# Weight conversion and input splitting moved from VectorE to GpSimd in a fused attention + two-MLP kernel

## The chip, the cores and the metric

One NeuronCore of a Trainium2 chip runs the whole program. The metric is the device time of one execution in microseconds; the table below has the median of three. The engines are named as in the profile: PE (TensorE matmuls) with PEld (its weight loads), DVE (VectorE), ACT (ScalarE), POOL (GpSimd) and SP, which issues the DMAs. Each engine works off its own queue strictly in the order in which the program was written; engines wait for one another through semaphores.

## The reference

Three stages, each fed by the one before; 3072 tokens of 384 features.

```
attention: y_t = q_t S;  S += beta_t k_t (v_t - S k_t)      # 4 batches x 8 heads, 768 steps
first MLP:  h = x @ w_in          # 384 -> 2048
            g = (a0 + a1 h + a2 h^2 + a3 h^3) / (1 + |b0||h| + |b1| h^2 + 1e-6)
            x = g @ w_out         # 2048 -> 384
second MLP: h = x @ w_in2;  out = (h tanh(softplus(h))) @ w_out2
```

The MLP weights arrive as 64-bit floats and have to be converted on the chip.

## The kernel before, in words

Tokens are kept in six groups of 512. An MLP is a sequence of **units**: one unit is one group (512 tokens) times one slice of 128 hidden features, so each MLP has 6 x 16 = 96 units, numbered 0 to 95 in the first MLP and on from 96 in the second. Units 16, 32, 48, 64 and 80 begin a new group. Products are formed from two parts of each number, a high part in the fast fp32r format and the remainder ("low half"), so a unit is 9 matmuls up (L893) and 9 down (L1002).

In the first MLP the work of unit u between its two matmul blocks is a chain over three engines. With the letters of the list that orders it:

- 1a (ACT, L924): q = |h|, read from PSUM; 1c (ACT, L933): s = a3 h + a2.
- 1b: r = b1 q + b0. On POOL (L927) for the units in `m1.pool`, else on ACT (L931).
- 1d (POOL, L937): q = q r, the denominator less 1.
- 1e, 1f (ACT, L945 and L947): r = exp(-ln(q + 1 + 1e-6)), its reciprocal; ACT issues them in the next unit's round, just ahead of 1a of that unit.
- 1g, 1h (DVE, L952 and L954): s = (s h + a1) h. 1h is the last reader of h and frees its PSUM buffer; there are two, so the up matmuls of unit u+2 wait for 1h of unit u.
- 1i, 1j, 1k (DVE, L961 to L970): the quotient g; 1L (ACT, L904) its high part; 1m (POOL, L908) its low part.

One round of the loop writes, for all engines, the list

```
"fx fw y0 y1 1e 1f u0 u1 u2 1a 1b 1c 1i 1j 1k 1d 1g 1h y2 d0 d1 d2 d3 xa 1L 1m xB f c",
```

where y0 to y2 copy a finished group's three sums out of PSUM (ACT, L1124, in the round of units 20, 36, 52, 68 and 84), xa and xB split the next group's input x into its high (ACT, L873) and low half (L877), fx loads it, and c and f advance the conversion of the second MLP's weights, a step here and there. A side (half) of a weight slice goes through these steps: its magnitude on ACT (L739, `mag`), a clamp (L744) and a shift (L748) on DVE (`size`), sign and low word on DVE (`sign` L754, `low` L760), then the high part on ACT (L767, `out`) and the remainder on POOL (L772, `rest`). The first 16 sides are converted during units 7 to 88 of the first MLP, one step in a unit, in the units listed in `calm`. A magnitude is put into the queue in the round after the `size` of the side before; `out` and `rest` in the round after `low`. The order on POOL at a round's end is 1m, then xB if POOL has it, then what f flushes.

The functions that the diff touches:

Of the kernel before, what the change touches and what calls it, by code (L numbers as in the profile page):

```python
# [9 lines left out]
F32 = mybir.dt.float32  # L10
F32R = mybir.dt.float32r
I32 = mybir.dt.int32
I64 = mybir.dt.int64
ACTF = mybir.ActivationFunctionType
ALU = mybir.AluOpType
# [27 lines left out]
CONV_START, CONV_RATE = 6, 4  # L43
# [650 lines left out]
class Weights:  # L694
# [5 lines left out]
    LEAST = 2.0 ** -15  # L700
    MOST = 1.875 * 2.0 ** 16
    free = False
    word = None

    def __init__(self, nc, w_in, w_out, sb, kept, passing, scratch):
# [14 lines left out]
    def convert(self, f, side):  # L720
        nc = self.nc
        w = {}

        def get():
            w["raw"] = self.sb.tile([128, 3, 128], I64, "w64")
            src = self.w_out[f * 128:(f + 1) * 128] if side else self.w_in[:, :, f * 128:(f + 1) * 128]
            nc.sync.dma_start(out=w["raw"], in_=src)

        def word(i):
            return w["raw"].rearrange("p k c -> p (k c)").bitcast(I32).rearrange("p (n t) -> p n t", t=2)[:, :, i]  # L730

        def mag():
            w["m"] = self.sb.tile([128, 384], I32, "wm")
            if self.free:
                nc.vector.tensor_scalar(
                    out=w["m"], in0=word(1), scalar1=0x7FFFFFFF, scalar2=None, op0=ALU.bitwise_and
                )
            else:
                nc.scalar.activation(out=w["m"].bitcast(F32), in_=word(1).bitcast(F32), func=ACTF.Abs)  # L739

        def size():
            m = w["m"]
            w["x"] = m if self.word is None else self.word.bitcast(I32)
            nc.vector.tensor_scalar(  # L744
                out=w["x"].bitcast(F32), in0=w["m"].bitcast(F32), scalar1=self.LEAST, scalar2=self.MOST,
                op0=ALU.max, op1=ALU.min,
            )
            nc.vector.tensor_scalar(  # L748
                out=w["x"], in0=w["x"], scalar1=3, scalar2=0x3FFFFFF8,
                op0=ALU.logical_shift_left, op1=ALU.bitwise_and,  # L750
            )

        def sign():
            nc.vector.scalar_tensor_tensor(  # L754
                out=w["x"], in0=word(1), scalar=-(1 << 30), in1=w["x"],
                op0=ALU.bitwise_and, op1=ALU.bitwise_or,
            )

        def low():
            nc.vector.scalar_tensor_tensor(  # L760
                out=w["m"], in0=word(0), scalar=29, in1=w["x"],
                op0=ALU.logical_shift_right, op1=ALU.bitwise_or,
            )

        def out():
            m = w["m"].bitcast(F32).rearrange("p (k c) -> p k c", k=3)
            nc.scalar.copy(out=self.tile(f)[:, 0, side], in_=m)  # L767

        def rest():
            t = self.tile(f)  # L770
            m = w["m"].bitcast(F32).rearrange("p (k c) -> p k c", k=3)
            nc.gpsimd.tensor_tensor(out=t[:, 1, side], in0=m, in1=t[:, 0, side].bitcast(F32), op=ALU.subtract)  # L772

        def done():
            if side and f in self.tag:
                self.store(f)

        return get, mag, size, sign, low, out, rest, done

    def plan(self, p, fs):  # L780
# [265 lines left out]
def tile_delta_attention_two_mlps(  # L1046
# [14 lines left out]
    nc = tc.nc  # L1061
# [24 lines left out]
    units = [(g, f) for g in range(NG) for f in range(NF)]  # L1086
    n1 = len(units)
    units += [(g, f) for g in range(NG) for f in range(NF)]
    n2 = len(units)
# [3 lines left out]
    w2 = Weights(nc, moe2_w_in, moe2_w_out, sb, (), range(DIRECT), wd[1])  # L1093
    def run(fns):
        for fn in fns:
            fn()
# [3 lines left out]
    m1 = Mlp1(nc, w1, sb, ps, x1, consts)  # L1100
    m2 = Mlp2(nc, w2, sb, ps, x2, consts)

    def mlp(i):
        return m1 if i < n1 else m2

    def starts(i):
        return i == 0 or i == n1 or units[i][0] != units[i - 1][0]
# [70 lines left out]
    with ExitStack() as bctx:  # L1178
        sb2 = bctx.enter_context(tc.tile_pool(name="sb2", bufs=1, reuse_waits="tile"))
        ps2 = bctx.enter_context(tc.tile_pool(name="ps2", bufs=1, space=PSUM, reuse_waits="tile"))  # L1180
        sb.add(sb2, w=NF - FQ - FG, wt=1, w64=1, wm=1, x=1, q=3, s=3, r=2, g=3, gh=5 - FIRST, ev=3)
        ps.add(ps2, h=2, o=4, r=2)
        own = FQ + FG
        fetch_w = {n: (w1.fetch_split, own + LOOK + n) for n in range(NF - own - LOOK)}
        for f in range(DIRECT):
            fetch_w[n1 - NF + 6 + f] = (w2.fetch_split, f)
        calm = [i for i in range(CONV_START, n1 - 8) if not any(starts(i + 5 - k) for k in range(3))]
        for f in range(LOOK):
            w1.fetch_split(own + f)
        steps = [  # L1190
            (m1, "1a", m1.e1, [0]), (m1, "1b", m1.e1, [1]), (m1, "1c", m1.e1, [2]), (m1, "1d", m1.e2, None),
            (m1, "1e", m1.e3, [0]), (m1, "1f", m1.e3, [1]), (m1, "1g", m1.e4, [0]), (m1, "1h", m1.e4, [1]),
            (m1, "1i", m1.e5, [0]), (m1, "1j", m1.e5, [1]), (m1, "1k", m1.e5, [2]),
            (m1, "1l", m1.hi, "V"), (m1, "1L", m1.hi, "A"), (m1, "1P", m1.hi, "P"),
            (m1, "1m", m1.lo, "P"), (m1, "1M", m1.lo, "V"),
            (m2, "2a", m2.e1, None), (m2, "2b", m2.e2, None), (m2, "2M", m2.lo, None),
        ]
        steps = {name: (m, f, a) for m, name, f, a in steps}
        ups, downs = {}, {}
        m1.pool = {i for i in range(n1) if i % 2 or any(starts(j) for j in range(i + 3, i + 6) if j < n2)}  # L1200
        m2.pool = range(n1, n1 + NF)
        for i in range(n2 + max(LG.values())):
            kind = int(i >= n1)
            if i == CONV_START - 3:
                conv.start()

            def at_x(f):
                for k in range(3):
                    j = i + 5 - k
                    if 0 < j < n2 and starts(j):  # L1210
                        f(mlp(j))(units[j][0], k)

            for op in LISTS[kind]:
                if op in steps:
                    m, f, a = steps[op]
                    j = i - LG[op[0] + {"L": "l", "P": "l", "M": "m"}.get(op[1], op[1])]
                    if FIRST <= j < n2 and mlp(j) is m:
                        f(j, *([a] if a else []))
                elif op[0] == "u" and FIRST <= i < n2:
                    if i not in ups:  # L1220
                        ups[i] = mlp(i).up(i, *units[i])
                    n = int(op[1])
                    run(ups[i][3 * n:3 * n + 3])
                elif op[0] == "d" and 0 <= i - FIRST < FIRST:
                    if i - FIRST not in downs:
                        downs[i - FIRST] = down(i - FIRST)
                    n = int(op[1])
                    run(downs[i - FIRST][0][3 * n:3 * n + 3])
                elif op[0] in "dvy" and FIRST <= i - LAG - (op[0] == "y") < n2:
                    j = i - LAG - (op[0] == "y")  # L1230
                    if j not in downs:
                        downs[j] = down(j)
                    n = int(op[1])
                    if op[0] == "d":
                        run(downs[j][0][3 * n:3 * n + 3])
                    elif (op[0] == "y") == (j < n1):
                        run(downs[j][1][n:n + 1])
                elif op == "fw" and i in fetch_w:
                    fetch, f = fetch_w[i]
                    fetch(f)  # L1240
                elif op == "fx" and i + 8 < n2 and starts(i + 8):
                    mlp(i + 8).fetch_x(units[i + 8][0])
                elif op == "xa":
                    at_x(lambda m: m.x_hi)
                elif op == "xB":
                    at_x(lambda m: lambda g, k: m.x_lo(g, k, "V"))
                elif op == "c" and i > n1:
                    w2.free = True
                    w2.word = w2.word or ps.tile([128, TOK], F32, "r")[:, 0:384]
                    conv.pull(CONV_RATE)  # L1250
                elif op == "c" and i in calm:
                    conv.pull(6 * DIRECT * (calm.index(i) + 1) // len(calm) - conv.n)
                elif op == "f":
                    conv.flush()
# [29 lines left out]
```

## Time and profile before

| | before |
|---|---|
| median of 3 runs | 1126.9 us (1125.48 to 1130.12) |
| profiled execution | 1126.43 us |
| its span, first to last instruction | 1124.7 us |
| PE, DVE, ACT, POOL busy over the span | 1060.0, 720.8, 610.8, 541.2 us |

The profiled execution's own time is 1.7 us above its span, which lies before the first and behind the last instruction. Attention fills the first 319 us, the first MLP reaches to about 726 us, the second from there to the end. In the first MLP DVE is busy more than nine tenths, ACT and POOL between seven and nine tenths; in the second DVE, ACT and POOL are mostly idle and PE is busy throughout.

### The profile page before, as it was taken

What the parts mean: (1) busy time and instruction counts of PE and PEld (TensorE: products, weight loads), DVE (VectorE), ACT (ScalarE), POOL (GpSimd) and SP (SyncE); (2) the same over time, 40 slices, a digit from 0 to 9 for tenths busy, and PEclk for the clock granted to TensorE, in tenths of its full rate; (3) what the DMA queues carried; (4) which work ended last, traced back from release to release, by engine and by line L of the source; (5) the groups of instructions that cost most, each with busy time, mean ns of one, the idle gap of its engine ahead of it and who ended that gap; (6) DMA issues with size and microseconds to landing.
All of it is one profiled execution on the core that took longest, in us unless ns stands there. A gap on an engine that the chain in (4) does not pass through costs nothing.

```text
span 1124.7 us, 24637 instructions
## 1 busy us (share of the span) xinstructions
PE 1060.0 (94%) x10172; PEld 920.8 (82%) x10172; DVE 720.8 (64%) x1207; ACT 610.8 (54%) x1100; POOL 541.2 (48%) x623
## 2 busy tenths in 40 slices
PE   6778988798989999999999999999999999999998
PEld 5668877688868778878887887899999999999997
DVE  5996577995669999999999999992121211212110
ACT  4524455233568888988889888743333223233322
POOL 4287778667447777777777877763000000000000
PEclk8996899995899999999999999999999999999999
DMA  7616877234473021121202036250101001010000
GB/s 146 140 29 163 201 206 199 46 88 101 102 267 141 15 99 43 57 71 62 94 15 98 15 141 239 67 172 1 57 1 57 1 11 46 1 57 1 29 1 28
DMA packets 120111, 92.91 MB, mean 83 GB/s; under 512 B 79680, under 2 KB 104384, under 8 KB 120000
## 3 DMA queue, kind: packets, MB, share of 16 engines
q1 hardware_dynamic: 119744, 91.25, 27.7%
q8 instruction: 79, 1.29, 0.5%
q14 instruction: 32, 0.26, 0.1%
q0 software_dynamic: 256, 0.10, 0.1%
HBM read 63.02 MB, written 28.31 MB: 81 GB/s over the span
## 4 chain that ended last, share of the span: by engine, by line
PE 50%; POOL 15%; DVE 12%; ACT 12%; issue 7%; DMA 3%; SPq 2%; POOLq 0%; DVEq 0%; ACTq 0%
PE h L893 20%; PE o L1035 18%; POOL q L937 7%; POOL gh L908 3%; PE o L1002 3%; ACT r L945 3%; POOL r L927 3%; PE c_ps L597 2%; ACT q L924 2%; ACT r L947 2%; PE y_ps L635 2%; DVE tmp L520 1%; SPq L310 1%; PE c_ps L580 1%; PE s_all L620 1%
## 5 line engine op out<-in xcount | busy, mean ns | idle before, releaser
L893 PE MATMUL h<-x,w 128*128 128x512 f32 x1278 | 318.0, 393 | 3.9 <-DVE s L954 3.6
L893 PEld LDWEIGHTS h<-x,w 128*128 128x128 f32 x1278 | 237.0, 188 | 56.5 <-DVE s L954 10.2
L908 DVE TENSOR_TENSOR gh<-g,gh 128x512 fp32r<-128x512 f32 x80 | 55.3, 692 | 282.8 <-ACT g L1026 282.8
L1021 ACT ACTIVATE gh<-h 128x512 fp32r<-128x512 f32 x96 | 57.5, 599 | 231.4 <-PE h L893 231.4
L1035 PE MATMUL o<-w,gh 128*128 128x384 f32 x864 | 162.5, 337 | 0.0
L1002 PE MATMUL o<-gh,w 128*128 128x512 f32 x648 | 159.2, 390 | 0.0
L1035 PEld LDWEIGHTS o<-w,gh 128*128 128x128 f32 x864 | 153.4, 188 | 6.0
L908 POOL TENSOR_TENSOR gh<-g,gh 128x512 fp32r<-128x512 f32 x110 | 142.6, 1297 | 23.8 <-ACT g L1026 21.4
L937 POOL TENSOR_TENSOR q<-q,r 128x512 f32<-128x512 f32 x94 | 122.0, 1297 | 61.6 <-ACT r L931 57.2
L1002 PEld LDWEIGHTS o<-gh,w 128*128 128x128 f32 x648 | 121.5, 188 | 26.0 <-ACT ev L1124 0.8
L893 PE MATMUL h<-x,wg 128*128 128x512 f32 x432 | 107.0, 392 | 2.8 <-DVE wm L760 1.6
L893 PEld LDWEIGHTS h<-x,wg 128*128 128x128 f32 x432 | 80.5, 188 | 19.9 <-DVE s L954 2.5
L945 ACT ACTIVATE r<-q,cst 128x512 f32<-128x512 f32 x94 | 65.0, 692 | 48.8 <-POOL q L937 48.7
L933 ACT ACTIVATE s<-h,ab 128x512 f32<-128x512 f32 x94 | 72.7, 774 | 0.0
L954 DVE SCALAR_TENSOR_TENSOR s<-s,ab,h 128x512 f32<-128x512 f32 x94 | 70.2, 747 | 3.3
L961 DVE SCALAR_TENSOR_TENSOR q<-q,r 128x512 f32<-128x512 f32 x94 | 63.8, 679 | 13.4 <-ACT r L947 13.1
L965 DVE SCALAR_TENSOR_TENSOR r<-s,ab,r 128x512 f32<-128x512 f32 x94 | 70.1, 745 | 0.0
L526 POOL TENSOR_TENSOR xs<-xs,tmp 128x30 f32<-128x30 f32 (+14 forms) x120 | 63.1, 526 | 9.4
L952 DVE TENSOR_TENSOR s<-s,h 128x512 f32<-128x512 f32 x94 | 63.8, 679 | 4.6 <-ACT s L933 4.6
L970 DVE SCALAR_TENSOR_TENSOR g<-q,r 128x512 f32<-128x512 f32 x94 | 64.5, 687 | 3.2
L520 POOL TENSOR_TENSOR tmp<-xs 128x30 f32<-128x30 f32 (+14 forms) x120 | 59.2, 493 | 7.4
L904 ACT CAST gh<-g 128x512 fp32r<-128x512 f32 x94 | 58.5, 623 | 0.0
(157 smaller groups left out, 1696.7 us busy)
## 6 DMA issues: line engine op xcount, KB each, us to landing
w<-w SPq DMA_DIRECT2D x24, 768.0 KB, 7.0
w<-in_moe_w_in_dram SPq DMA_DIRECT2D x32, 384.0 KB, 3.6
w<-in_moe_w_out_dram SPq DMA_DIRECT2D x32, 384.0 KB, 3.3
xraw<-x SPq DMA_DIRECT2D x36, 256.0 KB, 4.1
w<-wt SPq DMA_DIRECT2D x8, 768.0 KB, 3.4
kn<-in_k_dram SPq DMA_DIRECT2D x48, 96.0 KB, 3.6
gh<-in_q_dram SPq DMA_DIRECT2D x48, 96.0 KB, 3.3
v<-in_v_dram SPq DMA_DIRECT2D x48, 96.0 KB, 3.9
```

What stands on the lines that cost most here:

```text
L520: eng.tensor_tensor(out=tv, in0=ls[:, j, j + 1:HC].unsqueeze(1).to_broadcast([128, j, n]), in1=xs[:, 0:j, j:j + 1].to_broadcast([128, j, n ...
L893: self.nc.tensor.matmul(out=self.st[i]["h"], lhsT=self.w.t[f][:, a, 0, k], rhs=self.x[g][:, b, k], start=(n == 0), stop=(n == 8),)
L908: (nc.gpsimd if engine == "P" else nc.vector).tensor_tensor(out=s["gh"][:, 1], in0=s["g"], in1=s["gh"][:, 0].bitcast(F32), op=ALU.subtract)
L933: nc.scalar.activation(out=s["s"], in_=s["h"], func=ACTF.Identity, scale=k["a3"], bias=k["a2"])
L937: nc.gpsimd.tensor_tensor(out=s["q"], in0=s["q"], in1=s["r"], op=ALU.mult)
L945: nc.scalar.activation(out=s["r"], in_=s["q"], func=ACTF.Ln, bias=k["c"])
L952: nc.vector.tensor_tensor(out=s["s"], in0=s["s"], in1=s["h"], op=ALU.mult)
L954: nc.vector.scalar_tensor_tensor(out=s["s"], in0=s["s"], scalar=k["a1"], in1=s["h"], op0=ALU.add, op1=ALU.mult)
L965: nc.vector.scalar_tensor_tensor(out=s["r"], in0=s["s"], scalar=k["a0"], in1=s["r"], op0=ALU.add, op1=ALU.mult)
L970: nc.vector.scalar_tensor_tensor(out=s["g"], in0=s["q"], scalar=2.0, in1=s["r"], op0=ALU.subtract, op1=ALU.mult, reverse0=True)
L1002: self.nc.tensor.matmul(out=self.acc[g][d], lhsT=self.w.t[f][:, a, 1, d], rhs=self.st[i]["gh"][:, b], start=(first and n == 0), stop=(last ...
L1035: self.nc.tensor.matmul(out=self.acc[g][t][:, 0:384], lhsT=self.st[i]["gh"][:, a, t * 128:(t + 1) * 128], rhs=self.w.t[f][:, b, 1].rearran ...
```

## The change

In the second MLP's weights, while they are converted during the first MLP (`ahead`), the clamp leaves DVE: POOL does it right behind the magnitude, in place, and `size` on DVE is the shift alone. The low halves of x for groups 1 to 5 of the first MLP go from DVE to POOL; they, and the high halves on ACT, stand in rounds 7, 5 and 3 ahead of the group's first unit (all odd) in place of 5, 4 and 3. POOL does 1b in odd units only; before it also did in units 12, 28, 44, 60, 76 and 92. x is loaded 12 units ahead in place of 8. `calm` now leaves out the two rounds in which sums are or have just been copied out (20 and 21, 36 and 37, ...), and no longer those in which x is split, so the conversion steps stand in other units than before. The first group's x and all of the second MLP (its first group's x, split in rounds 91 to 93, included) keep DVE and the old distances.

```diff
--- before.py
+++ after.py
@@ -700,6 +700,7 @@
     LEAST = 2.0 ** -15
     MOST = 1.875 * 2.0 ** 16
     free = False
+    ahead = False
     word = None
 
     def __init__(self, nc, w_in, w_out, sb, kept, passing, scratch):
@@ -737,16 +738,21 @@
                 )
             else:
                 nc.scalar.activation(out=w["m"].bitcast(F32), in_=word(1).bitcast(F32), func=ACTF.Abs)
+            if self.ahead:
+                clamp(nc.gpsimd, w["m"])
+
+        def clamp(engine, out):
+            engine.tensor_scalar(
+                out=out.bitcast(F32), in0=w["m"].bitcast(F32), scalar1=self.LEAST, scalar2=self.MOST,
+                op0=ALU.max, op1=ALU.min,
+            )
 
         def size():
-            m = w["m"]
-            w["x"] = m if self.word is None else self.word.bitcast(I32)
+            w["x"] = w["m"] if self.word is None else self.word.bitcast(I32)
+            if not self.ahead:
+                clamp(nc.vector, w["x"])
             nc.vector.tensor_scalar(
-                out=w["x"].bitcast(F32), in0=w["m"].bitcast(F32), scalar1=self.LEAST, scalar2=self.MOST,
-                op0=ALU.max, op1=ALU.min,
-            )
-            nc.vector.tensor_scalar(
-                out=w["x"], in0=w["x"], scalar1=3, scalar2=0x3FFFFFF8,
+                out=w["x"], in0=w["m"] if self.ahead else w["x"], scalar1=3, scalar2=0x3FFFFFF8,
                 op0=ALU.logical_shift_left, op1=ALU.bitwise_and,
             )
 
@@ -1184,7 +1190,7 @@
         fetch_w = {n: (w1.fetch_split, own + LOOK + n) for n in range(NF - own - LOOK)}
         for f in range(DIRECT):
             fetch_w[n1 - NF + 6 + f] = (w2.fetch_split, f)
-        calm = [i for i in range(CONV_START, n1 - 8) if not any(starts(i + 5 - k) for k in range(3))]
+        calm = [i for i in range(CONV_START, n1 - 8) if not any(starts(i - 4 - k) for k in range(2))]
         for f in range(LOOK):
             w1.fetch_split(own + f)
         steps = [
@@ -1197,18 +1203,22 @@
         ]
         steps = {name: (m, f, a) for m, name, f, a in steps}
         ups, downs = {}, {}
-        m1.pool = {i for i in range(n1) if i % 2 or any(starts(j) for j in range(i + 3, i + 6) if j < n2)}
+        m1.pool = range(1, n1, 2)
         m2.pool = range(n1, n1 + NF)
         for i in range(n2 + max(LG.values())):
             kind = int(i >= n1)
             if i == CONV_START - 3:
                 conv.start()
+                w2.ahead = True
 
             def at_x(f):
                 for k in range(3):
+                    j = i + 7 - 2 * k
+                    if 0 < j < n1 and starts(j):
+                        f(m1)(units[j][0], k)
                     j = i + 5 - k
-                    if 0 < j < n2 and starts(j):
-                        f(mlp(j))(units[j][0], k)
+                    if n1 <= j < n2 and starts(j):
+                        f(m2)(units[j][0], k)
 
             for op in LISTS[kind]:
                 if op in steps:
@@ -1238,14 +1248,16 @@
                 elif op == "fw" and i in fetch_w:
                     fetch, f = fetch_w[i]
                     fetch(f)
-                elif op == "fx" and i + 8 < n2 and starts(i + 8):
-                    mlp(i + 8).fetch_x(units[i + 8][0])
+                elif op == "fx":
+                    for j in ((i + 12,) if i + 12 < n1 else ()) + ((i + 8,) if n1 <= i + 8 < n2 else ()):
+                        if starts(j):
+                            mlp(j).fetch_x(units[j][0])
                 elif op == "xa":
                     at_x(lambda m: m.x_hi)
                 elif op == "xB":
-                    at_x(lambda m: lambda g, k: m.x_lo(g, k, "V"))
+                    at_x(lambda m: lambda g, k: m.x_lo(g, k, "P" if m is m1 else "V"))
                 elif op == "c" and i > n1:
-                    w2.free = True
+                    w2.free, w2.ahead = True, False
                     w2.word = w2.word or ps.tile([128, TOK], F32, "r")[:, 0:384]
                     conv.pull(CONV_RATE)
                 elif op == "c" and i in calm:
```

How the instructions move, in two places. POOL, from 1d of unit 11 on (wt and wm are weight tiles, x and xraw the split and the loaded input); before:

```order
L937 TENSOR_TENSOR q<-q,r 128x512
L908 TENSOR_TENSOR gh<-g,gh 128x512
L772 TENSOR_TENSOR wt<-wm,wt 128x384
L927 TENSOR_SCALAR r<-q,ab 128x512
L937 TENSOR_TENSOR q<-q,r 128x512
L908 TENSOR_TENSOR gh<-g,gh 128x512
```

The same place after the change, where all lines have larger numbers (1d L943, 1m L914, 1b L933, the low half L883, `rest` L778, the clamp L745):

```order
L943 TENSOR_TENSOR q<-q,r 128x512
L914 TENSOR_TENSOR gh<-g,gh 128x512
L883 TENSOR_TENSOR x<-xraw,x 128x512
L778 TENSOR_TENSOR wt<-wm,wt 128x384
L943 TENSOR_TENSOR q<-q,r 128x512
L914 TENSOR_TENSOR gh<-g,gh 128x512
L745 TENSOR_SCALAR wm<-wm 128x384
```

Ahead of 1d of unit 12 there stood a `rest` and 1b; now a low half of x and a `rest`, and 1b has gone to ACT. A clamp stands behind unit 12's 1m.

ACT, from 1a of unit 11 to 1e of unit 12 (q is written by 1a, s by 1c, gh by 1L); before:

```order
L924 ACTIVATE q<-h 128x512
L933 ACTIVATE s<-h,ab 128x512
L873 CAST x<-xraw 128x512
L904 CAST gh<-g 128x512
L767 CAST wt<-wm 128x384
L945 ACTIVATE r<-q,cst 128x512
L947 ACTIVATE r<-r 128x512
L924 ACTIVATE q<-h 128x512
L933 ACTIVATE s<-h,ab 128x512
L873 CAST x<-xraw 128x512
L904 CAST gh<-g 128x512
L945 ACTIVATE r<-q,cst 128x512
```

After the change, from 1a of unit 12 (L930) on:

```order
L930 ACTIVATE q<-h 128x512
L937 ACTIVATE r<-q,ab 128x512
L939 ACTIVATE s<-h,ab 128x512
L910 CAST gh<-g 128x512
L740 ACTIVATE wm<-w_4949 128x384
L951 ACTIVATE r<-q,cst 128x512
```

Unit 11 keeps its high half of x and its `out`; in unit 12 the high half is gone, and 1b and a magnitude have come.

Where the moved steps stand in units 6 to 94, which are 89, read off the same orders. The 15 low halves on POOL stand in units 9, 11, 13, 25, 27, 29 and so on. Of the 16 `rest`, eight stand in even units before (18, 22, 26, 38, 42, 80, 84, 88) and eight after (20, 26, 42, 46, 62, 66, 82, 88); of the eight in odd units four now stand directly behind a low half of x (11, 57, 73, 77). The 17 magnitudes, each with its clamp on POOL now, stand in even units seven times before (8, 50, 66, 70, 74, 82, 86) and eight times after (8, 12, 28, 32, 48, 52, 68, 74); of the nine in odd units two (43, 59) have a low half ahead of the clamp. The third copy of sums, y2, in the round of an even unit, shares that unit with an `out` in unit 84 before and in unit 20 after, and with a magnitude in units 52 and 68 after. The first two copies share an odd unit with a magnitude or an `out` in 19 and 35 before and in 35, 51 and 83 after.

## Rows read from the trace of the kernel before

**Rows 1.** Busy time by stretch: us, PE, PEld, DVE, ACT, POOL, clock, DMA

```profile
333.60:726.10 392.50, 389.14 (x1692) 315.50 (x1693) 373.11 (x557) 337.56 (x574) 298.70 (x258) 1.00 0.24 84
726.10:1124.70 398.60, 393.68 (x1981) 357.24 (x1980) 100.83 (x158) 125.93 (x241) 31.87 (x27) 1.00 0.11 35
```

**Rows 2.** Waits in 333.6 to 726.1: total us, times, longest

```profile
ACT r L945 <- POOL q L937: 46.1, 70, 1.3
PEld h L893 <- DVE s L954: 12.7, 22, 2.1
```

**Rows 3.** Timeline of PE: start, us, the up matmuls of two units

```profile
564.11 2.20 PE L893 MATMUL h<-x,w 128*128 128x512 f32 x9
...
568.18 2.20 PE L893 MATMUL h<-x,w 128*128 128x512 f32 x9
```

**Rows 4.** Timeline of ACT and POOL, units 62 and 63; idle time before in brackets

```profile
572.18 0.59 ACT L924 ACTIVATE q<-h 128x512 f32<-128x512 f32 x1
...
573.70 1.30 POOL L937 TENSOR_TENSOR q<-q,r 128x512 f32<-128x512 f32 x1 [1.52 <-ACT r L931]
...
576.25 0.59 ACT L924 ACTIVATE q<-h 128x512 f32<-128x512 f32 x1
...
577.02 0.77 POOL L927 TENSOR_SCALAR r<-q,ab 128x512 f32<-128x512 f32 x1 [0.77 <-ACT q L924]
```

**Rows 5.** Timeline of ACT: 1a of unit 6 and of unit 95

```profile
338.14 0.59 ACT L924 ACTIVATE q<-h 128x512 f32<-128x512 f32 x1
...
709.83 0.59 ACT L924 ACTIVATE q<-h 128x512 f32<-128x512 f32 x1
```

**Rows 6.** Timeline of ACT: 1a of units 50, 51, 52 and 53

```profile
522.48 0.60 ACT L924 ACTIVATE q<-h 128x512 f32<-128x512 f32 x1
...
526.66 0.59 ACT L924 ACTIVATE q<-h 128x512 f32<-128x512 f32 x1
...
530.83 0.59 ACT L924 ACTIVATE q<-h 128x512 f32<-128x512 f32 x1
...
535.05 0.60 ACT L924 ACTIVATE q<-h 128x512 f32<-128x512 f32 x1
```

**Rows 7.** Timeline of ACT: 1a of units 13 and 14

```profile
367.81 0.59 ACT L924 ACTIVATE q<-h 128x512 f32<-128x512 f32 x1
...
371.90 0.59 ACT L924 ACTIVATE q<-h 128x512 f32<-128x512 f32 x1
```

**Rows 8.** Timeline of ACT: 1a of units 23, 24 and of 26, 27, 28

```profile
409.56 0.59 ACT L924 ACTIVATE q<-h 128x512 f32<-128x512 f32 x1
...
414.07 0.59 ACT L924 ACTIVATE q<-h 128x512 f32<-128x512 f32 x1
...
422.32 0.59 ACT L924 ACTIVATE q<-h 128x512 f32<-128x512 f32 x1
...
426.47 0.60 ACT L924 ACTIVATE q<-h 128x512 f32<-128x512 f32 x1
...
430.75 0.59 ACT L924 ACTIVATE q<-h 128x512 f32<-128x512 f32 x1
```

**Rows 9.** Timeline of ACT: 1a of units 84 and 85

```profile
663.67 0.59 ACT L924 ACTIVATE q<-h 128x512 f32<-128x512 f32 x1
...
668.30 0.59 ACT L924 ACTIVATE q<-h 128x512 f32<-128x512 f32 x1
```

**Rows 10.** Groups of lines in 333.6 to 726.1: count, busy us, mean ns

```profile
L927 POOL TENSOR_SCALAR r<-q,ab 128x512 f32<-128x512 f32 x52 | 40.6, 781 | 32.0 <-ACT q L924 32.0
...
L772 POOL TENSOR_TENSOR wt<-wm,wt 128x384 fp32r<-128x384 f32 x16 | 17.6, 1101 | 0.0
L877 DVE TENSOR_TENSOR x<-xraw,x 128x512 fp32r<-128x512 f32 x18 | 16.4, 908 | 0.0
...
L744 DVE TENSOR_SCALAR wm<-wm 128x384 f32<-128x384 f32 x16 | 10.6, 664 | 0.0
```

**Rows 11.** Group 0's low half of x on POOL: min/median/max ns

```profile
L877 POOL TENSOR_TENSOR x<-xraw,x x3: 1268/1271/1272, 280.1 to 290.4; 128x512 fp32r<-128x512 f32 x3
```

More of the change, by code (lines that the diff above doesn't have):

```diff
@@ L739, in mag, with size @@
                 nc.scalar.activation(out=w["m"].bitcast(F32), in_=word(1).bitcast(F32), func=ACTF.Abs)
-        def size():
-            m = w["m"]
-            w["x"] = m if self.word is None else self.word.bitcast(I32)
-            nc.vector.tensor_scalar(
-                out=w["x"].bitcast(F32), in0=w["m"].bitcast(F32), scalar1=self.LEAST, scalar2=self.MOST,
+            if self.ahead:
[3 more added lines that the diff above has]
+                out=out.bitcast(F32), in0=w["m"].bitcast(F32), scalar1=self.LEAST, scalar2=self.MOST,
                 op0=ALU.max, op1=ALU.min,
             )
+        def size():
+            w["x"] = w["m"] if self.word is None else self.word.bitcast(I32)
+            if not self.ahead:
+                clamp(nc.vector, w["x"])
             nc.vector.tensor_scalar(
-                out=w["x"], in0=w["x"], scalar1=3, scalar2=0x3FFFFFF8,
+                out=w["x"], in0=w["m"] if self.ahead else w["x"], scalar1=3, scalar2=0x3FFFFFF8,
                 op0=ALU.logical_shift_left, op1=ALU.bitwise_and,
```

## The prediction

> **What bounds the kernel now.** I first ask where time can be gained at all. By the stretches, the second MLP keeps PE busy 393.7 of 398.6 us, at a granted clock of 1.00, with all other engines mostly idle [rows 1]: nothing that happens there moves the end. The first MLP is the place: PE has 3.4 us idle in 392.5, but idle is not all that it loses. A unit's up matmuls begin 4.08 us apart where nothing holds them [rows 3], and 89 units of that are 363.1 us. How long did 89 units take?
>
> The list of waits names two suspects for the first MLP. PE's weight loads wait for 1h on DVE, 22 times, 12.7 us [rows 2], and DVE is busy 373.1 of 392.5 us [rows 1]. That reads as if DVE were the bound. But the same list has ACT waiting for POOL's 1d 70 times, 46.1 us [rows 2], on a chain that also repeats in each unit: 1a, 1b, 1d, 1e, 1f, and only then, since ACT's queue is in order, 1a of the next unit. To tell the two apart I read the starts of 1a. In an even unit, with 1b on ACT, the next 1a comes after 4.07 us [rows 4]; in an odd one, with 1b on POOL, after 4.17 (unit 51 to 52, [rows 6]). The mean, 4.12, is above PE's 4.08, so the chain alone is slower than PE. From 1a of unit 6 to 1a of unit 95 it takes 371.7 us [rows 5] for 89 units, 4.18 each, which is 8.6 us above PE's 363.1. In each of these 89 intervals 1a follows the end of 1f directly; none is ended by h from PE or by anything on DVE. So the reader should see in DVE's 12.7 us an echo: 1h trails a chain that is late by itself, and PE trails 1h. DVE's own delays shift a stall of PE by a unit or two and are then absorbed, because PE can regain 0.09 us where the chain cannot.
>
> So I count what the change does to this chain, in units 6 to 94.
>
> **The chain before, as base and extras.** Base: 39 even units with 1b on ACT at 4.07 us; 38 units with 1b on POOL behind such a unit at 4.17; and 12 units with 1b on POOL behind another such unit, which take 4.09 [rows 7]. Sum 158.7 + 158.5 + 49.1 = 366.3. Measured 371.7, so conversion, splitting and copies now cost the chain 5.4 us. Their prices, where a row isolates one:
> - A magnitude in an even unit: 4.18 against 4.07, 0.11 (unit 50 to 51, [rows 6]). In odd units ACT has room: unit 51, with two copies of sums, takes the plain 4.17 [rows 6].
> - y2 in an even unit: 4.22, 0.15 [rows 6]; y2 with an `out`: 4.63, 0.56 [rows 9].
> - `out` and `rest` in an even unit: that unit 4.15 (0.08), the next 4.28 (0.11; units 26 and 27, [rows 8]), together 0.19; with a two-step `size` on DVE alongside, the next takes 4.51 (unit 23, [rows 8]), together 0.42.
>
> **Removed from DVE.** 16 clamps, 10.6 us, and 15 of 18 low halves, 15 x 0.908 = 13.6 us [rows 10]: 24 us of DVE. I credit the chain with nothing for them. DVE's queue still decides how soon 1h follows 1a, but the end comes from the last unit where PE waits, and there (units 92 to 94) DVE still splits x as before. What hides this work is the chain itself; with a faster chain it would count, up to the 8.6 us above.
>
> **Base after.** 45 even units at 4.07, 44 odd at 4.17: 183.2 + 183.5 = 366.6, 0.3 more than before, because the pairs of POOL units at 4.09 are gone.
>
> **Added to POOL: low halves of x.** One takes 1.27 us there [rows 11]. In an undisturbed pair POOL finishes 1m of the odd unit just as the even unit's 1a begins (idle 1.52 us up to 573.70, so from 572.18, where 1a starts) [rows 4]. So a low half at an odd unit's end falls into a gap of 1.52 us and by itself costs nothing, with 0.25 to spare: nine of the fifteen stand so. Four have a `rest` behind them, mean 1.10 us [rows 10]: 1.27 + 1.10 - 1.52 = 0.85 late for 1d of the even unit, 3.4 us in all. This is the largest term. Two have a clamp behind them: with the clamp at 0.59 (below), 1.27 + 0.59 - 1.52 = 0.34, 0.7 in all.
>
> **Added to POOL: clamps.** The trace has none on POOL. The nearest row is 1b there, also one input and two scalar operations, 0.781 us for 512 columns [rows 10]; for 384 I take three quarters, 0.59. Lower bound: nothing. Upper bound: the price of a two-input step of 384 columns, 1.10 [rows 10]. In an odd unit it has the 1.52 gap. In an even one POOL is idle 0.77 us before the next 1b [rows 4], so 0.59 fits at no cost; at 1.10 it would not, by 0.33. VectorE waits for a clamp only at the very first `size`, which was put right behind its magnitude; that can delay 1h of unit 8 by about 1 us, once, and PE regains it.
>
> **Moved by `calm`.** Eight `rest` in even units before, eight after. After: unit 20 shares its y2 with an `out`, 0.6; the seven others cost 0.19 (four, no `size` alongside) or between that and 0.42 (three, the shift alone alongside; I take 0.30): 1.7. y2 with a magnitude in units 52 and 68: I take the 0.56 of y2 with `out` plus 0.04 for the longer step, 1.2. Magnitudes in 8, 28, 32 and 48: 0.4; in 12 and 74 they hide behind the late 1d. y2 alone in 36 and 84: 0.3. Three odd units with a weight step and two copies: at most y2's 0.15 each, 0.4. Unit 92, now with 1b on ACT and a high half of x there: 0.2.
>
> **x loaded sooner.** The DMAs go past one weight fetch, for a unit eleven places on; x is used five units later. Nothing waits for either in the rows; zero, and if the weight were late, it would stall PE once at unit 15.
>
> **Sum.** Extras after: 3.4 + 0.7 + 0.6 + 1.7 + 1.2 + 0.4 + 0.3 + 0.4 + 0.2 = 8.9 us. Change: 8.9 - 5.4 + 0.3 = +3.8 us. Against the profiled execution that is 1126.43 + 3.8 = 1130.2; the median of the runs lies 0.5 above it. I take **1130.5 us**, 0.3% more: less than the 0.5% (5.6 us) that a measurement of this kernel can tell from no change.
>
> **A rule beside the rows.** The same subtraction takes 0.908 us on DVE in this stretch and 1.27 on POOL [rows 10, 11]. The Trainium skill (GPSIMD Engine Reference, Engine selection) calls POOL about two times slower for two-input elementwise steps and about line rate for one input. By its factor the low half would be an estimated 1.8 us and each of the fifteen would outgrow the 1.52 gap: nine by 0.3 and the six crowded ones by 0.55 more than above, some 6 us on top, 1136. The trace has POOL at 1.4 times, and I go by the trace.
>
> **Rivals.**
> 1. *DVE does bind* (faster). For: 12.7 us of waits name it and it is 95% busy. Against: 1a never waits for it in 89 units. If PE really ran behind DVE alone, the loss above PE's pace, 8.6 us, could go: 1117.8 at best, about 1122 with half. It decides where a 1a starts later than the end of 1f. Chance 0.10.
> 2. *The gaps take everything* (no change). If 1d's wait has more room than the two units that I read, the six crowded places cost nothing: 8.9 - 4.1 = 4.8 us of extras, -0.3 in all, 1126.2 to 1126.6. Against: in rows 4 the gap is closed by ACT's 1b, a fixed step. Chance 0.13.
> 3. *POOL's steps are dearer* (slower). Clamps at 1.10 us: six even units at 0.33 and two crowded ones at 0.51 more, 3.0 us. Every even `rest` at 0.42: 1.3. Sum 1130.5 + 4.3 = 1134.8. For: `rest` has a mean of 1.10 and unit 23 shows 0.23 more than unit 27 when DVE's tensor-scalar steps lie alongside. Against: the change takes half of those steps away. Chance 0.15. The Trainium skill (SBUF, Who interferes with whom) has a cause that would press this way: VectorE and GpSimd share a port pair, and the second to start is blocked until the first ends. By that rule more POOL work meets DVE's shifts; the spread of the rows agrees.
>
> **Range and chances.** The forecast has 0.62. Its own range is 1128.5 to 1132.5 (extras 7 to 11). To hold 8 in 10 the range reaches rival 2 and most of rival 3: 1125.8 to 1134.0. Faster by over 0.5% (below 1121.3): 0.09, rival 1; slower by over 0.5% (above 1132.5): 0.17, most of rival 3 and the forecast's upper edge; within: 0.74.
>
> **What would show it.** In the changed kernel: 1a to 1a still 4.07 and 4.17 in plain units, and 1a behind 1f everywhere; units 12, 58, 74 and 78 at about 4.9; 44 and 60 at about 4.4; 52 and 68 at about 4.7; DVE busy some 24 us less in the first MLP with PE's total hardly moved; POOL's clamp near 0.6 us. I am wrong if 1a begins to wait for PE or DVE, if low half plus `rest` does not delay 1d, or if clamps take over 0.77 us.

## The result, and the profile after

The changed kernel takes 1139.2 us, median of 6 runs (1133.1 to 1145.8), against 1127.0 for the kernel before; the ratio is 1.0117, 95% interval 1.007 to 1.0164. The forecast was 1130.5 with a range to 1134.0: the time lies outside it, on the slow side. Slower was the direction; the amount, 12.2 us, is more than three times the 3.8 that I had. The execution of e4 that was profiled, used below, is a slow one of its kernel, but from 345 to 700 us its granted clock is 1.00 as in the others, so that stretch can be compared.

The profiled execution takes 1138.44 us, 12.0 more than that of before. The chain of the prediction is the place to look first. Timeline of ACT in the changed kernel, 1a (now L930) of unit 6 and of unit 95:

```profile
338.91 0.59 ACT L930 ACTIVATE q<-h 128x512 f32<-128x512 f32 x1
...
722.04 0.59 ACT L930 ACTIVATE q<-h 128x512 f32<-128x512 f32 x1
```

That is 383.1 us for the same 89 units that took 371.7 [rows 5]: +11.4, where the whole execution differs by 12.0; 0.8 had come before unit 6, and what differs behind unit 95 is under 0.5. From the first down matmul of the second MLP to the last instruction both kernels take 393.0 us. So the loss is the chain's.

The stretch and the waits of the first MLP (columns as in [rows 1, 2]), and the groups on POOL (count, busy us, mean ns, as in [rows 10]):

```profile
334.40:738.50 404.10, 395.63 (x1692) 312.80 (x1693) 359.54 (x526) 342.77 (x580) 340.24 (x284) 1.00 0.23 82
```

```profile
ACT r L951 <- POOL q L943: 52.2, 71, 2.0
DVE q L967 <- ACT r L953: 35.4, 42, 1.9
...
PEld h L899 <- DVE s L960: 27.9, 55, 2.1
```

```profile
L933 POOL TENSOR_SCALAR r<-q,ab 128x512 f32<-128x512 f32 x46 | 35.5, 773 | 22.2 <-ACT q L930 22.2
L745 POOL TENSOR_SCALAR wm<-wm 128x384 f32<-128x384 f32 x17 | 26.9, 1582 | 0.0
L883 POOL TENSOR_TENSOR x<-xraw,x 128x512 fp32r<-128x512 f32 x15 | 22.1, 1475 | 0.0
L778 POOL TENSOR_TENSOR wt<-wm,wt 128x384 fp32r<-128x384 f32 x16 | 17.0, 1061 | 0.0
```

DVE is busy 13.6 us less than before and yet PE's loads wait for its 1h more than twice as long: 27.9 us where it was 12.7 [rows 2]. DVE now waits itself, 35.4 us, for 1f on ACT, which waits for 1d on POOL; in the kernel before that wait of DVE was 11.8:

```profile
DVE q L961 <- ACT r L947: 11.8, 20, 1.0
```

And the clamp, L745, takes 1.58 us in the mean, where the prediction took 0.59 and put the upper bound at 1.10. It has the longest mean of all groups on POOL, with fewer columns than any but `rest`.

What one clamp does is seen in two places of the timeline (start, us). Units 59 to 61, a low half and a clamp in one gap:

```profile
567.38 0.59 ACT L930 ACTIVATE q<-h 128x512 f32<-128x512 f32 x1
...
571.50 1.62 POOL L883 TENSOR_TENSOR x<-xraw,x 128x512 fp32r<-128x512 f32 x1
...
571.56 0.60 ACT L930 ACTIVATE q<-h 128x512 f32<-128x512 f32 x1
...
573.10 1.49 POOL L745 TENSOR_SCALAR wm<-wm 128x384 f32<-128x384 f32 x1
...
574.55 1.29 POOL L943 TENSOR_TENSOR q<-q,r 128x512 f32<-128x512 f32 x1
...
577.09 0.59 ACT L930 ACTIVATE q<-h 128x512 f32<-128x512 f32 x1
```

1d of unit 60 starts 2.99 us behind its 1a where 1.52 is the plain distance [rows 4]; the unit takes 5.53 us in place of 4.07. Units 28 to 30, a clamp at the end of an even unit:

```profile
437.02 1.80 POOL L745 TENSOR_SCALAR wm<-wm 128x384 f32<-128x384 f32 x1
...
437.15 0.59 ACT L930 ACTIVATE q<-h 128x512 f32<-128x512 f32 x1
...
438.80 0.77 POOL L933 TENSOR_SCALAR r<-q,ab 128x512 f32<-128x512 f32 x1
...
442.20 0.60 ACT L930 ACTIVATE q<-h 128x512 f32<-128x512 f32 x1
```

1b of unit 29 could start 0.77 us behind its 1a [rows 4], but POOL is in the clamp until 1.65 behind it, and the unit takes 5.05 us in place of 4.17.

### The profile page after: what moved, and what is told of

The parts are those of the page before. It is cut to its first block, busy times and chain, and to the rows that moved or that the text cites. A ratio compares the mean times of both kernels' runs of the same rounds, so it can differ in the third digit from the quotient of the medians.

```text
span 1136.7 us, 24632 instructions
## 1 busy us (share of the span) xinstructions
PE 1064.4 (94%) x10172; PEld 916.8 (81%) x10172; DVE 707.4 (62%) x1176; ACT 616.4 (54%) x1106; POOL 582.9 (51%) x649
## 4 chain that ended last, share of the span: by engine, by line
PE 48%; POOL 19%; DVE 11%; ACT 10%; issue 6%; DMA 3%; SPq 1%; POOLq 0%; DVEq 0%; ACTq 0%
PE h L899 19%; PE o L1041 18%; POOL q L943 8%; POOL gh L914 5%; PE y_ps L635 3%; POOL r L933 3%; ACT r L951 2%; PE c_ps L597 2%; PE o L1008 2%; ACT r L953 2%; ACT q L930 2%; POOL x L883 1%; POOL wm L745 1%; DMA w<-in_moe_w_in_dram 1%; DVE tmp L520 1%
## 5 line engine op out<-in xcount | busy, mean ns | idle before, releaser
L914 DVE TENSOR_TENSOR gh<-g,gh 128x512 fp32r<-128x512 f32 x80 | 55.4, 693 | 282.7 <-ACT g L1032 282.7
L914 POOL TENSOR_TENSOR gh<-g,gh 128x512 fp32r<-128x512 f32 x110 | 142.8, 1299 | 24.5 <-ACT g L1032 21.6
L943 POOL TENSOR_TENSOR q<-q,r 128x512 f32<-128x512 f32 x94 | 122.2, 1300 | 41.0 <-ACT r L937 35.2
L778 POOL TENSOR_TENSOR w<-wm,w 128x384 fp32r<-128x384 f32 x40 | 41.8, 1048 | 35.6 <-ACT w L773 35.5
```

What stands on the lines that cost most here:

```text
L914: (nc.gpsimd if engine == "P" else nc.vector).tensor_tensor(out=s["gh"][:, 1], in0=s["g"], in1=s["gh"][:, 0].bitcast(F32), op=ALU.subtract)
L943: nc.gpsimd.tensor_tensor(out=s["q"], in0=s["q"], in1=s["r"], op=ALU.mult)
```

## The experiments

Theory A: the chain 1a, 1b, 1d, 1e, 1f bounds the first MLP, because ACT's queue lets no unit's 1a go ahead of the last unit's 1f; what POOL puts between is paid in full, and what leaves DVE is worth nothing there. Theory B: the low halves on POOL and the new places of the steps make the loss. Theory C: DVE binds after all.

The second column is the ratio to the kernel before, measured beside it, with its interval; the third is 1a of unit 6 to 1a of unit 95 in the profile, the fourth 1a of unit 6 to the first down matmul of the second MLP, all in us.

| kernel | ratio, 95% | 6 to 95 | 6 to second MLP |
|---|---|---|---|
| before | 1 | 371.7 | 390.1 |
| changed | 1.0117 (1.007 to 1.0164) | 383.1 | 401.7 |
| e1: clamps back on DVE | 1.0033 (1.0011 to 1.0056) | 376.0 | 394.5 |
| e12: low halves back on DVE | 1.0031 (0.9992 to 1.0069) | 377.8 | 396.4 |
| e5: clamps on POOL, cheap operations | 1.0037 (1.0004 to 1.007) | 375.1 | 393.7 |
| e10: e1, steps out of the splitting rounds | 1.0028 (1.0003 to 1.0054) | 374.8 | 393.4 |
| e2: before, clamps on POOL | 1.0077 (1.0041 to 1.0112) | 379.9 | 398.3 |
| e4: before, 1a moved | 1.0015 (0.9977 to 1.0052) | 375.5 | 395.7 |
| e8: e4, 1g and 1h moved too | 1.0119 (1.0046 to 1.0192) | 383.7 | 404.2 |
| e6: changed, 1a moved | 0.9954 (0.992 to 0.9988) | 367.9 | 388.1 |
| e7: e1, 1a moved | 1.0034 (1.0 to 1.0068) | 374.6 | 394.8 |
| e11: e6, steps out of the splitting rounds | 0.9966 (0.9934 to 0.9998) | 365.2 | 385.4 |
| e13: e11 again | 0.9953 (0.9918 to 0.9987) | 365.4 | 385.6 |

In every one of these profiles the second MLP takes 393.0 us from its first down matmul on. What differs outside the table is the time up to unit 6, where 1a starts between 323.7 and 341.8 us; that is attention, where these kernels are the same, and the first units.

**e1, the clamps given back.**

```diff
-                w2.ahead = True
+                w2.ahead = False
```

> The changed kernel with the clamps given back to VectorE (the shift and all else as changed). Theory A, the chain 1a-1b-1d-1e-1f bounds and the clamp on GpSimd is what the prediction sized wrong: the chain from 1a of unit 6 to 1a of unit 95 falls from 383.1 us to 374 to 375.5, time +2 to +4 us against the kernel before (ratio 1.002 to 1.0035); units 44 and 60 at 4.07 to 4.2 in place of 5.23 and 5.53; unit 12 stays near 4.8, because the remainder behind the low half stays. Theory B, the low halves on GpSimd and the new places of the conversion steps are the loss: stays at 1.008 or more. Theory C, VectorE binds: about as fast as the changed kernel or slower, since VectorE gets 10 us more.

376.0 us, -7.1 from the changed kernel, and 1.0033: theory A, half a microsecond above its interval. What is left against the kernel before, 4.3 us, is all that B can have. C is out for this order of ACT: DVE has 10 us more to do and the kernel is faster. Timeline of e1, units 60 and 61:

```profile
565.42 1.62 POOL L883 TENSOR_TENSOR x<-xraw,x 128x512 fp32r<-128x512 f32 x1
565.48 0.60 ACT L930 ACTIVATE q<-h 128x512 f32<-128x512 f32 x1
567.01 1.30 POOL L943 TENSOR_TENSOR q<-q,r 128x512 f32<-128x512 f32 x1
...
569.57 0.60 ACT L930 ACTIVATE q<-h 128x512 f32<-128x512 f32 x1
```

A low half alone, even at 1.62 us, still fits the gap: 1d starts at 1.53, the unit takes 4.09.

**e2, only the clamps.** The kernel before, with `mag`, `clamp` and `size` of the changed kernel and `ahead` set as there.

> The kernel before with the clamps alone moved to GpSimd. Theory A: seven magnitudes in even units leave GpSimd 0.7 to 1.0 us late for the next unit's 1b, two more (units 43, 59) run into a unit with 1b on GpSimd, so the chain grows by 6 to 8 us and the time by as much (ratio 1.005 to 1.007). Theory C, VectorE binds: 10.6 us less on VectorE, time falls (0.992 to 0.998). Theory B: the same time as before.

379.9 us, +8.2, and 1.0077: A, both numbers a little above what was expected. Alone, the clamps cost more than all the rest of the change together (4.3 us, e1).

**e3, the price by itself.** In the second MLP, where POOL is idle, steps on a scratch tile:

```diff
+            if i == n1 + 24:
+                pa, pb = sb.tile([128, TOK], F32, "q"), sb.tile([128, TOK], F32, "s")
+                nc.gpsimd.memset(pa, 1.5)
+                g = nc.gpsimd
+                for _ in range(3):
+                    g.tensor_scalar(out=pb[:, 0:384], in0=pa[:, 0:384], scalar1=Weights.LEAST, scalar2=Weights.MOST, op0=ALU.max, op1=ALU.min)
...
```

> The kernel before with 24 extra GpSimd steps of the tensor-scalar kind in the second MLP, where GpSimd is idle; they write to a scratch tile and change no output. Three each of: clamp (max, min with constants) on 384 columns; multiply, add with constants on 384; multiply, add with scalars from a tile on 384, and on 512; max, min with scalars from a tile on 384; max alone on 384; multiply alone on 384; max, min with constants on 512. If the kind of operation makes the clamp slow: max, min at 1.45 to 1.5 us here too, multiply, add near 0.6. If sharing with a busy VectorE makes it slow: max, min below 0.8 us here. If constants in place of tile scalars make it slow: multiply, add with constants at 1.5 too. Time of the program unchanged.

The instructions of these lines (minimum, median, maximum ns), in the order named there:

```profile
L1209 POOL TENSOR_SCALAR s<-q x3: 1490/1497/1502, 775.1 to 778.3; 128x384 f32<-128x384 f32 x3
L1211 POOL TENSOR_SCALAR s<-q x3: 515/518/519, 779.9 to 781.1; 128x384 f32<-128x384 f32 x3
L1213 POOL TENSOR_SCALAR s<-q,ab x3: 667/670/1153, 781.7 to 783.7; 128x384 f32<-128x384 f32 x3
L1215 POOL TENSOR_SCALAR s<-q,ab x3: 772/773/1083, 784.5 to 786.2; 128x512 f32<-128x512 f32 x3
L1217 POOL TENSOR_SCALAR s<-q,ab x3: 1641/1644/1647, 787.4 to 790.9; 128x384 f32<-128x384 f32 x3
L1219 POOL TENSOR_SCALAR s<-q x3: 1167/1176/1277, 792.6 to 795.3; 128x384 f32<-128x384 f32 x3
L1221 POOL TENSOR_SCALAR s<-q x3: 1171/1171/1177, 796.5 to 799.0; 128x384 f32<-128x384 f32 x3
L1223 POOL TENSOR_SCALAR s<-q x3: 1917/1918/1927, 800.3 to 804.3; 128x512 f32<-128x512 f32 x3
```

It is the kind of operation. The clamp takes 1.50 us beside a nearly idle DVE as well; multiply and add on the same columns 0.52. The starts say the same without the durations: from the first to the third start, 3.2 us for the clamps and 1.2 for multiply and add. Constants or scalars from a tile change 0.15 us. In passing: multiply alone takes 1.17, more than twice multiply and add together. The chain of this kernel, 372.2 us, also shows how well the quantity repeats.

**e5, the same step at about the price that was forecast.** The clamp itself is left out here: the step on POOL multiplies by 1 and adds 0.

```diff
-                out=out.bitcast(F32), in0=w["m"].bitcast(F32), scalar1=self.LEAST, scalar2=self.MOST,
-                op0=ALU.max, op1=ALU.min,
+                out=out.bitcast(F32), in0=w["m"].bitcast(F32),
+                **(dict(scalar1=1.0, scalar2=0.0, op0=ALU.mult, op1=ALU.add) if self.ahead else
+                   dict(scalar1=self.LEAST, scalar2=self.MOST, op0=ALU.max, op1=ALU.min)),
```

> The changed kernel with max, min of GpSimd's clamp replaced by multiply by 1, add 0 (the clamp is left out, the step on GpSimd stays). Its step costs 0.52 us by the probe, near the 0.59 that the prediction took. If the clamp's price is all that the prediction missed: chain from 1a of unit 6 to 1a of unit 95 at 374.3 to 375.7 us, time +3 to +4 against the kernel before (ratio 1.0025 to 1.004), units 44 and 60 near 4.4. If more work on GpSimd of any price hurts by sharing with VectorE: chain above 378.

375.1 us, +3.4, ratio 1.0037; the forecast was +3.8 and 1.003. Timeline of e5, unit 60 again:

```profile
565.58 1.61 POOL L884 TENSOR_TENSOR x<-xraw,x 128x512 fp32r<-128x512 f32 x1
565.63 0.60 ACT L931 ACTIVATE q<-h 128x512 f32<-128x512 f32 x1
567.17 0.52 POOL L745 TENSOR_SCALAR wm<-wm 128x384 f32<-128x384 f32 x1
...
570.19 0.59 ACT L931 ACTIVATE q<-h 128x512 f32<-128x512 f32 x1
```

4.56 us, where the prediction had about 4.4; unit 44, of the same kind, takes 4.26. The other reading on record, that more work on POOL hurts at any price, falls with this: it hurts by its length and place.

**e12, the low halves given back.** `"P" if m is m1 else "V"` becomes `"V"`.

> The changed kernel with the low halves given back to VectorE (clamps on GpSimd, places of all steps as changed). If the long clamps cost by themselves only in even units (0.6 to 0.9 us for each of eight) and the rest of the loss is their meeting with low halves: chain from 1a of unit 6 to 1a of unit 95 at 376 to 379 us (383.1 in the changed kernel, 371.7 before), time +4 to +7 us (ratio 1.004 to 1.0065). If the low halves cost nothing: 382 or more.

377.8 us, as A has it; the ratio, 1.0031, is below what was expected, with an interval that reaches from no change to +0.7%. By the chain, giving back either part gains 7.1 or 5.3 us, together more than the 11.4 there are: where a clamp and a low half meet, both are needed for the loss. Unit 60 takes 5.53 us with both, 4.09 without the clamp (e1) and 4.42 without the low half (e12).

**e10, low halves uncrowded.** e1, with

```diff
-        calm = [i for i in range(CONV_START, n1 - 8) if not any(starts(i - 4 - k) for k in range(2))]
+        calm = [i for i in range(CONV_START, n1 - 8) if not any(starts(i + d) for d in (-4, -5, 4, 6, 8))]
```

> e1_clamp_back (clamps on VectorE, low halves on GpSimd) with the conversion steps kept out of the rounds in which x is split, so that all 15 low halves stand alone in GpSimd's gap ahead of an even unit's 1d. If low halves are free there and only the crowding costs: the four late units of 0.65 to 0.8 us go, chain from 1a of unit 6 to 1a of unit 95 at 372.5 to 374.5 us against 376.0 in e1_clamp_back and 371.7 before. If a low half on GpSimd costs by itself: 376 or more.

374.8, just above the interval of "free". The four late units behind a low half and a `rest` (3.1 us over their plain times in e1) are gone, and no unit behind a low half is late by more than a magnitude's 0.11. But the chain gains only 1.2 us: the steps now meet y2 in more places (units 20, 36, 52, 68 and 84 at 4.63 to 4.67; in e1 units 36 and 84 take 4.23), and the other moved steps cost about as much again. A shifted step costs where it lands.

**e4, the chain loosened.** ACT's 1a ahead of the last unit's 1e and 1f:

```diff
-    "fx fw y0 y1 1e 1f u0 u1 u2 1a 1b 1c 1i 1j 1k 1d 1g 1h y2 ...",
+    "fx fw y0 y1 u0 u1 u2 1a 1e 1f 1b 1c 1i 1j 1k 1d 1g 1h y2 ...",
```

> The kernel before with one entry of the first MLP's list moved: 1a of a unit now stands ahead of 1e and 1f of the unit before in ScalarE's queue, so the chain no longer has to end before the next begins. Theory A: units come at PE's 4.08 to 4.10 us, the first MLP loses 6 to 9 us, 1118 to 1121 us (ratio 0.992 to 0.995). Theory C, VectorE binds: same time within 2 us, with PE's loads still waiting for 1h.

No gain: the time is the same within its interval, and in the profile the stretch is 5.6 us longer. A's number fails, C's holds. Waits of e4 from 335 to 735 us, and its DVE and PE at one of PE's stalls (idle time before, and what ended it, in brackets):

```profile
ACT q L924 <- PE h L893: 51.6, 66, 2.0
PEld h L893 <- DVE s L954: 18.5, 20, 2.2
...
PE h L893 <- DVE s L954: 10.9, 15, 1.7
...
ACT r L945 <- POOL q L937: 0.3, 1, 0.3
```

```profile
379.83 0.72 DVE L744 TENSOR_SCALAR wm<-wm 128x384 f32<-128x384 f32 x1
380.58 1.34 DVE L748 TENSOR_SCALAR wm<-wm 128x384 int32<-128x384 int32 x1
...
385.35 2.33 PE L893 MATMUL h<-x,w 128*128 128x512 f32 x9 [0.75 <-DVE s L954]
```

The chain is loosened: ACT's wait for POOL's 1d falls from 46.1 us [rows 2] to 0.3, and 1a now waits for PE. But right behind it stands DVE: a two-step `size` of 2.1 us in one unit, in a queue whose five steps of a unit take some 3.5 of 4.08 us, holds 1h back, and PE with it. Long stretches run at 4.08 us a unit, broken by such stalls. So A is right for the kernel as it stands and C for the next bound.

**e6, the changed kernel with 1a moved** (the same edit).

> The changed kernel, clamps on GpSimd and all, with 1a ahead of 1e and 1f in the list, as in e4_reorder. There VectorE bound, in bursts where it does a conversion step. If that is so, VectorE's 24 us less are now worth something, and GpSimd (some 3.7 us of work in a unit of 4.08) may be late without holding ScalarE: from 1a of unit 6 to the first down matmul of the second MLP 385 to 390 us against 390.1 before and 395.7 in e4_reorder; time 0 to 5 us below the kernel before. If low halves and clamps on GpSimd are bad in any order: 394 or more.

388.1 us against 395.7 in e4, ratio 0.9954: faster than before. By the profiles, the same change that costs 11.6 us in the old order of ACT (401.7 - 390.1) gains 7.6 in the new one (395.7 - 388.1); the ratios, 1.0015 for e4 and 0.9954, differ by as much, though their intervals overlap a little. PE's loads wait 6.9 us for 1h in place of 18.5:

```profile
PEld h L899 <- DVE s L960: 6.9, 18, 1.0
...
PE h L899 <- DVE s L960: 1.4, 4, 0.6
```

**e7, which part gains.** e1 with 1a moved.

> e1_clamp_back (low halves on GpSimd, clamps on VectorE) with the same move of 1a. VectorE gets 10 us more than in e6_after_reorder and GpSimd 27 less. If VectorE's bursts bind once the chain is loosened: 2 to 6 us slower than e6_after_reorder. If GpSimd's long clamps bind: 2 to 6 us faster.

394.8, 6.7 slower than e6, a little more than expected, and the intervals of the two ratios are apart. With the chain loosened nearly all the gain comes with the clamps, the very part that cost most before: the rest of the change alone brings 0.9 (395.7 to 394.8). No run moves the clamps alone in this order.

**e8, 1h ahead of the quotient.** e4 with `1g 1h` ahead of `1i 1j 1k`.

> The kernel before with 1a ahead of 1e and 1f, and in VectorE's queue 1g and 1h of a unit ahead of 1i to 1k of the unit before, so that PE's buffer is freed before the quotient. If in e4_reorder VectorE's bursts bind through 1h: most of PE's stalls go, from 1a of unit 6 to the first down matmul of the second MLP 384 to 388 us, 2 to 6 us below the kernel before. If VectorE's total binds: 393 or more, as in e4_reorder.

404.2 us and 1.0119: a miss, slower than either side had a reason for. In the waits the place where it shows is ACT's 1L, which now waits for the quotient, 47.5 us in all:

```profile
ACT gh L904 <- DVE g L970: 47.5, 50, 2.4
```

The reading that fits: 1g and 1h, some 1.4 us, stand ahead of the quotient in DVE's queue, so 1L comes late, and the next unit's 1a stands behind 1L in ACT's queue. That 1g itself waits for ACT's 1c is the smaller part, 5.4 us in 11 waits. No run tests this reading.

**e11 and e13, the best found.** e6 with the `calm` of e10.

> e6_after_reorder (the changed kernel with 1a moved) with the conversion steps kept out of the rounds in which x is split. GpSimd's heaps of a low half and a remainder or a clamp go, but VectorE's steps stand closer together elsewhere. If GpSimd's heaps cause what PE still loses there: from 1a of unit 6 to the first down matmul of the second MLP 385 to 387 us (388.1 in e6_after_reorder). If VectorE's bursts do: 388 to 391.

> e11_reorder_not_crowded again, with more rounds, as the version that should beat both: ratio 0.993 to 0.998 against the kernel before; from 1a of unit 6 to the first down matmul of the second MLP 384 to 388 us.

385.4 and 385.6 us; 1119.4 us, ratio 0.9953 (0.9918 to 0.9987) with more rounds. That is where the first reading put them: a low half and a step piled up on POOL were part of what e6 still lost. In the stretch from 334 to 720 us PE is busy 385.8 of 386.0:

```profile
334.00:720.00 386.00, 385.82 (x1695) 316.53 (x1695) 353.96 (x530) 339.60 (x582) 337.83 (x283) 1.00 0.24 83
```

What remains there to gain is little: 365.2 us where 89 units at PE's 4.08 are 363.1. Whether its ratio differs from that of e6 the intervals do not tell.

## Why the prediction was wrong, step by step

**What bounds: right.** The chain grew by 11.4 us and the profiled execution by 12.0. Relief of DVE alone was no gain in this order of ACT (e1, e2), and in the changed kernel each 1a again starts 0.09 us ahead of the recorded end of the last 1f.

**Added to POOL, clamps: the step that failed.** The prediction took 0.59 us from 1b, "also one input and two scalar operations", three quarters of it, and bounded it by the 1.10 of a two-input step. The first is a multiply and an add, the second a subtraction; the clamp is max and min, and takes 1.48 to 1.80. The sign of the term was not the trouble, its price was: at 0.59 it fits the 0.77 us of an even unit's end, at 1.5 it does not. Summed over the units of the changed kernel, as over their plain times: behind eight even units 5.3 us (forecast 0), behind the two low halves 2.6 (0.7), behind three clamps near 1.80 in odd units and the first one 0.7 (0). That is 8.6 where 0.7 stood, and 7.9 is slightly more than the whole error of the chain, 383.1 - 375.5 = 7.6. An upper bound taken from the nearest rows has to be of the same kind of operation; no row of before had a max or a min on POOL, so the bound was not one, and the range that came from it was too narrow.

**Low halves with a `rest` behind: right.** Units 12, 58, 74 and 78 take 4.73 to 4.87, 2.9 us over in all (forecast 3.4, "about 4.9"). **Low halves alone: right**, in the gap, though at 1.30 to 1.62 us and not 1.27; e1 shows that 1.62 still fits.

**`calm`: right**: 1.7 for `rest` in even units (1.7), 1.2 for y2 with a magnitude (1.2), 0.6 for unit 20 (0.6), 0.4 for magnitudes (0.4). **Base: right**, 4.07 and 4.17. **x loaded sooner: right**, unit 15 takes 4.17. PE's busy time, which was to hardly move, reads 395.6 us against 389.1 for the same 1692 matmuls; the chain does not hang on it. **DVE's relief: overstated**, 13.6 us less busy and not 24: `sign`, `low` and the shift went from 11.9, 15.0 and 11.3 us to 17.0, 14.3 and 12.6, which is 5.7 of the 10.6 that are missing; the rest no row isolates. In this order it made no difference.

**The rivals.** DVE binding was out for this order, and true for the next one (e4): its condition, "where a 1a starts later than the end of 1f", is what the moved 1a brings about. Dearer POOL steps was the rival that came, by the operation and not by the meeting with DVE that I had given as its reason; e3 has the same 1.50 us where DVE is nearly idle. The meeting exists but is the smaller part: 0.3 us of the five clamps at 1.80, and of the seven low halves at 1.61 to 1.62, all with DVE's `sign` or `low` still running as they begin. In e5 the cheap step takes 0.81 to 0.83 us in the same five units and 0.51 to 0.53 elsewhere, the same 0.3 whatever the operation. Unit 28, whose clamp at 437.02 is shown above, and unit 8:

```profile
436.55 0.92 DVE L760 SCALAR_TENSOR_TENSOR wm<-w,wm 128x384 int32<-128x384 int32 x1
```

```profile
351.39 1.49 POOL L745 TENSOR_SCALAR wm<-wm 128x384 f32<-128x384 f32 x1
...
352.31 0.55 DVE L760 SCALAR_TENSOR_TENSOR wm<-w,wm 128x384 int32<-128x384 int32 x1
```

The Trainium skill (SBUF, Who interferes with whom) says that a DVE step with two inputs in SBUF, the on-chip memory, contends with a GpSimd step that reads SBUF; `sign` and `low` are such steps. The trace agrees where `sign` is already running as the clamp begins (unit 28, 1.80 us); where `sign` begins 0.92 us into the clamp (unit 8), neither is longer.

**The rule beside the rows.** The Trainium skill (GPSIMD Engine Reference, Engine selection) has one-input steps on GpSimd at roughly line rate. The runs show no single rate: 1.50 us for max and min on 384 columns is 3.9 ns a column, 0.52 for multiply and add 1.35. The measurement decides. The 1136 us that the prediction worked out from that section's factor for two-input steps lies nearer to the measured time, by luck: it had each low half take 1.8 us and outgrow its gap, and none took over 1.63.

## What to carry to other kernels

When two engines hand work back and forth in order, time the round trip before the engines: here 1a to 1a at 4.18 us named the bound that DVE's 95% busy share hid. Work taken off an engine that only trails such a loop gains nothing and costs whatever it adds to the loop; loosen the loop first and measure the same change again, since its sign may turn. And a price carried over from another instruction has to share its operation, not only its shape.

## What the runs showed of the hardware

A tensor-scalar step on GpSimd depends strongly on the operation: for 384 columns 0.52 us for multiply and add with constants, 0.67 with scalars from a tile, 1.17 for one multiply or one max alone, 1.50 for max and min. So one operation alone costs more than twice the pair of multiply and add.

The runs of a kernel scatter by more than one part in a hundred (before: 1113.9 to 1130.2 in one set), while the first MLP's chain repeats within 0.6 us (371.7 and 372.2 for the same instructions there, 365.2 and 365.4) and the second MLP within 0.03. In the profiles the scatter is in the time up to unit 6, and at its two ends the clock granted to PE in attention differs. From 200 to 300 us it is 0.98 in e12, where 1a of unit 6 comes earliest, at 323.7 us, and 0.83 in e4, where it comes latest, at 341.8 (stretch, busy times, clock, DMA, as in [rows 1]; e12, then e4):

```profile
200.00:300.00 100.00, 85.53 (x2649) 76.99 (x2647) 85.62 (x151) 44.34 (x87) 68.16 (x101) 0.98 0.34 86
```

```profile
200.00:300.00 100.00, 89.17 (x2317) 81.03 (x2315) 75.20 (x138) 36.24 (x73) 60.79 (x95) 0.83 0.33 81
```

From 345 to 700 us, in the first MLP, it is 1.00 in both. Why it differs in attention, where the kernels are the same, no run here shows.
